# Choosing ScalarE's pair of score tiles from the heads that VectorE's open quad does not need

## The chip, the cores and the metric

The kernel runs on one core of a Trainium2 chip. The metric is device time in microseconds (us) of one execution; the time before is the median of five executions. A profile is one execution recorded by the hardware profiler: it has a time of its own, and a span from its first to its last instruction.

## The reference

Two independent results stand side by side in the output, each 2048 x 640. The first is a spectral filter: a two-dimensional real FFT, a product with complex weights, and the inverse. The second is softmax attention with 32 heads of 20 columns:

```python
X = rfft2(x); y = irfft2(X * (w_r + 1j * w_i))            # output columns 0..639
q, k, v = split(x @ wqkv)                                  # S=2048, D=640, H=32, Dh=20
p = softmax(einsum("bhqd,bhkd->bhqk", q, k) * Dh ** -0.5)
b = einsum("bhqk,bhkd->bhqd", p, v).reshape(B, S, D) @ wo  # output columns 640..1279
```

## The kernel before

**Tiles of the attention.** A unit is one group of four heads (g, 8 of them) and 512 queries (qc, 4 of them): 32 units, worked through in the order of UNITS. Within a unit, one score tile is 128 keys (kt, 16 of them) by 512 queries of one head (j, 0 to 3), one PSUM bank in float32. There are 32 x 16 x 4 = 2048 such tiles. The four tiles of one unit and one kt are called a quad here. A head has 20 columns padded to 32 partitions, so the four heads of a quad lie on four different 32-partition row groups of TensorE, and tiles of different j can be multiplied at the same time (score_mm, L814 to L817).

**Two engines take exponentials.** ScalarE takes tiles in pairs: one ACTIVATE over two neighbouring banks (L1413) makes 128 x 1024 float16 values in a ring of 14 slots. VectorE makes an approximation by integer arithmetic: each tile is clamped from PSUM to int16 (L950, called p1); once the four tiles of its quad are there, two passes over 128 x 2048 (L993, p2, and L992, p3) make two shifted copies, which are read as float16. The values of that quad are scaled once for this (L1000, 128 x 96, called vs). All tiles of a VectorE quad must be from one quad (the assertion at L998).

**PSUM.** Banks 0 and 1, and 2 and 3, are the two sets that ScalarE's pairs alternate between (SETS). Banks 4 to 7 are shared by VectorE's tiles, the accumulator of the value product, and the matmuls of everything else.

**TensorE.** It writes scores (L816: three forms of call: a pair for ScalarE, tiles for VectorE that ride in the same call window as a pair, and tiles for VectorE alone), value products (L1071: four 32-column matmuls side by side are a wave, one wave for each ScalarE quad and three for each VectorE quad), and the background: projections, the filter's stages (L1738, L1821, L1925, L1977) and the output projection (L1217). A value product is only written when all four tiles of a quad are there (pv_waves, L1013).

**The order of the work.** It is decided while the program is built. Class KB walks through a simulated time with a cost for each instruction; at each step every free engine takes what is ready (run, L1574). What comes out are five fixed lists of instructions, one for each engine, with semaphore waits; on the chip each engine works through its list in order. For TensorE the first choice is always ScalarE's next pair (try_act_fill, L864). It takes the pair from pick_set (L793): first the remaining tiles of quads that ScalarE has opened (aq), then new quads. Then, while VectorE has little queued (dve_wants, L925: less than 2.0 us of work, 1.6 us for a second tile, and not all of the shared banks taken), up to two of VectorE's tiles ride along, as far as their heads differ from those of the pair:

```python
            dt = self.pick_dve_tile(set(t[2] for t in tiles), dts)
...
        if self.dq:
            for t in self.dq:
                if t[2] not in bad_j and all(t[2] != d[0][2] for d in dts):
                    return t
            return None
```

Here dq holds the remaining tiles of the quad that VectorE has opened, t[2] is the head, and bad_j are the heads of ScalarE's pair. So a VectorE quad with, say, only heads 0 and 1 left cannot go on beside a pair of heads 0 and 1. Lone VectorE tiles are written by try_dve_fill (L1457) when TensorE has room.

Of the kernel before, what the change touches and what calls it, by code (L numbers as in the profile page):

```python
# [297 lines left out]
class KB:  # L298
# [565 lines left out]
    def try_act_fill(self):  # L864
        if self.ua >= NU:
            return False
        banks = self.SETS[self.grp]
        if any(self.bank_owner[b] is not None for b in banks):
            return False
        if len(self.sets) >= 2:  # L870
            return False
        if self.P.peek("pe", w=[("ps", b) for b in banks]) > self.now:
            return False
        tiles = self.pick_set(len(banks))
        if not tiles:
            return False
        left = sum(4 * len(q) for q in self.qs[self.ua:self.ua + 2]) + len(self.aq)
        if len(tiles) < len(banks) and left > len(tiles) and self.act_started and not self.starved():
            return False
        for t in tiles:  # L880
            self.take_tile(t)
        bl = banks[:len(tiles)]
        rk = set()
        for u, kt, j in tiles:
            rk.update(self.kq_keys(u, kt))
        dts = []
        while len(tiles) + len(dts) < 4 and self.dve_wants(len(dts)):
            db = self.free_bank()
            if db is None:
                break  # L890
            dt = self.pick_dve_tile(set(t[2] for t in tiles), dts)
            if dt is None:
                break
            dts.append((dt, db))
            self.dve_take(dt, db)
        wk = [("ps", b) for b in bl]

        def fn(e):
            inst = None
            for (u, kt, j), b in zip(tiles, bl):  # L900
                inst = self.score_mm(e, u, kt, j, b)
            return inst
        n = len(tiles)
        self.put("pe", fn, 216.0 + 4.0 * (n - 1), r=list(rk), w=wk, name="fillA", mode="S")
        for b in bl:
            self.bank_owner[b] = "act"
        self.sets.append((tiles, bl, self.grp))
        self.grp ^= 1
        self.act_started = True
        self.act_tiles += n  # L910
        for dt, db in dts:
            self.dve_fill(dt, db, 4.0)
        return True
# [1314 lines left out]
```

## Time and profile before

| what | us |
|---|---|
| median of five executions (758.14 to 759.6) | 758.99 |
| the profiled execution, its own time | 756.96 |
| its span | 755.2 |
| busy: PE 722.2, ACT 729.6, DVE 674.3, POOL 132.7 | |
| first exponential of ScalarE starts | 12.52 |
| last exponential of ScalarE ends | 743.5 |

PE is TensorE's matmuls, PEld its weight loads, ACT is ScalarE, DVE VectorE, POOL GpSimd, SP the engine that issues most transfers. Busy time is the union of the recorded instructions of an engine. A recorded instruction can overlap the next one of its engine, so the step from one start to the next, called the pitch below, can be shorter than the recorded duration. Idle time is put down to what ended it. The granted clock of TensorE was 1.00 throughout.

### The profile page before, as it was taken

What the parts mean: (1) busy time and instruction counts of PE and PEld (TensorE: products, weight loads), DVE (VectorE), ACT (ScalarE), POOL (GpSimd) and SP (SyncE); (2) the same over time, 40 slices, a digit from 0 to 9 for tenths busy, and PEclk for the clock granted to TensorE, in tenths of its full rate; (3) what the DMA queues carried; (4) which work ended last, traced back from release to release, by engine and by line L of the source; (5) the groups of instructions that cost most, each with busy time, mean ns of one, the idle gap of its engine ahead of it and who ended that gap; (6) DMA issues with size and microseconds to landing.
All of it is one profiled execution on the core that took longest, in us unless ns stands there. A gap on an engine that the chain in (4) does not pass through costs nothing.

```text
span 755.2 us, 16333 instructions
## 1 busy us (share of the span) xinstructions
PE 722.2 (96%) x6488; PEld 232.0 (31%) x6537; DVE 674.3 (89%) x1259; ACT 729.6 (97%) x797; POOL 132.7 (18%) x141
## 2 busy tenths in 40 slices
PE   8999999999999999999999999999999999999997
PEld 4422332423322222232223333322222233333233
DVE  3698999999899999999988899999898998898995
ACT  5899999999999999999999999999999999999995
POOL 7398740000000100003020021100000000000000
PEclk9999999999999999999999999999999999999999
DMA  9022331102012126013010111130010211111101
GB/s 312 23 69 86 103 97 41 40 7 61 22 37 55 49 74 230 22 47 116 18 49 11 56 51 38 24 110 21 21 46 19 89 36 55 38 52 37 43 20 39
DMA packets 43504, 44.67 MB, mean 59 GB/s; under 512 B 16741, under 2 KB 36583, under 8 KB 43167
## 3 DMA queue, kind: packets, MB, share of 16 engines
q1 hardware_dynamic: 42654, 42.25, 18.6%
q0 software_dynamic: 768, 1.32, 0.7%
q8 instruction: 53, 0.87, 0.5%
q14 instruction: 29, 0.23, 0.1%
HBM read 28.47 MB, written 8.36 MB: 49 GB/s over the span
## 4 chain that ended last, share of the span: by engine, by line
ACT 63%; PE 26%; DVE 9%; issue 1%; DVEq 0%
ACT arena L1413 63%; PE ps L816 9%; PE ps L1071 7%; DVE arena L950 3%; PE ps L1821 2%; PE ps L649 2%; PE ps L1217 2%; PE ps L698 1%; DVE arena L992 1%; PE ps L620 1%; DVE arena L993 1%; DVE arena L1853 1%; DVE arena L1000 1%; PE ps L1977 1%; PE ps L1738 1%
## 5 line engine op out<-in xcount | busy, mean ns | idle before, releaser
L1413 ACT ACTIVATE arena<-ps 128x1024 f16<-128x1024 f32 x784 | 722.4, 1117 | 9.1 <-PE ps L816 7.4
L950 DVE TENSOR_SCALAR arena<-ps 128x512 int16<-128x512 f32 x480 | 320.3, 682 | 32.0 <-PE ps L816 28.4
L816 PE MATMUL ps<-arena 32*128 32x512 bf16 x2048 | 308.7, 384 | 13.8 <-ACT arena L1413 8.9
L1071 PE MATMUL ps<-arena 128*32 128x512 f16 x3008 | 235.5, 385 | 3.0 <-DVE arena L1000 1.0
L816 PEld LDWEIGHTS ps<-arena 32*128 32x128 bf16 x2048 | 76.3, 91 | 291.9 <-ACT arena L1413 268.3
L1123 POOL TENSOR_TENSOR arena<-arena 128x512 bf16<-128x512 f32 x30 | 40.4, 1348 | 512.3 <-DMA arena<-rd 512.3
L992 DVE TENSOR_SCALAR arena<-arena 128x2048 int16<-128x2048 int16 x120 | 89.4, 745 | 3.8 <-PE ps L1071 3.2
L993 DVE TENSOR_SCALAR arena<-arena 128x2048 int16<-128x2048 int16 x120 | 86.4, 720 | 0.6
L1071 PEld LDWEIGHTS ps<-arena 128*32 128x32 bf16 x3008 | 51.0, 94 | 97.3 <-issue 65.4
L649 PE MATMUL ps<-arena 128*128 128x512 bf16 x148 | 44.4, 383 | 2.6 <-issue 2.3
L1821 PE MATMUL ps<-arena 128*128 128x322 bf16 (+1 forms) x198 | 38.2, 304 | 0.7 <-issue 0.2
L1977 PE MATMUL ps<-arena 128*128 128x320 bf16 (+1 forms) x192 | 35.7, 302 | 0.0
L698 PE MATMUL ps<-arena 128*128 128x160 bf16 x320 | 31.5, 234 | 1.2 <-DVE arena L950 0.5
L1000 DVE TENSOR_SCALAR arena<-arena 128x96 bf16<-128x96 bf16 x120 | 31.2, 260 | 0.0
L1853 DVE TENSOR_TENSOR arena<-ps,arena 128x644 bf16<-128x644 f32 (+1 forms) x34 | 27.9, 821 | 3.2 <-PE ps L1821 2.8
L1925 PE MATMUL ps<-arena 128*128 128x512 bf16 (+3 forms) x122 | 29.2, 332 | 1.5 <-issue 1.4
L1217 PE MATMUL ps<-arena 128*128 128x320 bf16 (+1 forms) x152 | 28.8, 302 | 0.6 <-DVE arena L950 0.6
L698 PEld LDWEIGHTS ps<-arena 128*128 128x128 bf16 x320 | 21.3, 98 | 14.5 <-issue 9.8
L1102 DVE COPY arena<-ps 128x512 f32<-128x512 f32 (+1 forms) x33 | 21.9, 667 | 2.4 <-PE ps L1071 2.3
L661 DVE TENSOR_SCALAR arena<-ps 128x512 bf16<-128x512 f32 x34 | 23.2, 682 | 0.6 <-PE ps L649 0.4
L1738 PE MATMUL ps<-arena 128*128 128x512 bf16 x70 | 21.4, 383 | 1.6 <-issue 1.3
L704 DVE CAST arena<-ps 128x320 bf16<-128x320 f32 x32 | 15.5, 487 | 7.2 <-PE ps L698 7.1
(82 smaller groups left out, 366.9 us busy)
## 6 DMA issues: line engine op xcount, KB each, us to landing
arena<-rd SPq DMA_DIRECT2D x120, 64.0 KB
out_dram<-arena SPq DMA_DIRECT2D x32, 160.0 KB
arena<-in_A_x_dram SPq DMA_DIRECT2D x16, 160.0 KB
xs<-arena SPq DMA_DIRECT2D x16, 160.0 KB
arena<-xs SPq DMA_DIRECT2D x4, 640.0 KB
arena<-arena SPq DMA_DIRECT2D x105, 20.0 KB
arena<-ct SPq DMA_DIRECT2D x2, 1024.0 KB
arena<-ct SPq DMA_DIRECT2D x4, 512.0 KB
```

Source lines behind the costliest of these rows:

```text
L649: return lambda e: e.matmul(o, l, r_, start=(cc == 0), stop=(cc == 4))
L698: return lambda e: e.matmul(o, l, r_, start=st, stop=(c == 4), skip_group_check=True)
L816: return e.matmul(self.ps[:, bank, :], self.KT[32 * j:32 * j + 32, g, kt * 128:(kt + 1) * 128], self.QT[32 * j:32 * j + 32, g, qc * 512:(q ...
L950: return e.tensor_scalar(o, in_, 0.0, 31744.0, ALU.max, ALU.min)
L992: self.dve_push([(lambda e, en: e.tensor_scalar(Ii, Ii, SH2, 0.0, ALU.subtract, ALU.max), occ, ik + pk, ik, [], "p3")], lambda: push(self. ...
L993: ops = [(lambda e, en: e.tensor_scalar(Gi, Ii, SH1, 0.0, ALU.subtract, ALU.max), occ, ik, [("G", b)], [], "p2")]
L1071: inst = e.matmul(self.ps[32 * j:32 * j + 32, bank, :], v_, p_, start=s_, stop=False, tile_position=(0, 32 * j), skip_group_check=True)
L1123: self.pool_op(lambda e: e.tensor_tensor(on, of, bc, ALU.mult), 1600.0, r=pk + [("bcu", u, j) for j in range(4)] + [("bc", j) for j in ran ...
L1217: return lambda e: e.matmul(o, ot[0:M, c, qb * 128:(qb + 1) * 128], self.wo[0:M, c, half * 320:(half + 1) * 320], start=(c == 0), stop=(c ...
L1413: self.put("act", lambda e: e.activation(o, in_, AF.Exp, bias=ACT_BIAS, scale=ACT_SCALE), 0.8333 * 512 * n + 60.0, r=[("ps", b) for b in b ...
L1821: return lambda e: e.matmul(o, lhs, r_, start=st, stop=sp)
L1977: return lambda e: e.matmul(o, l, r_, start=(n == 0), stop=(n == 5))
```

## The change

Six lines go into try_act_fill, after a pair has been picked and before it is taken. If VectorE has an open quad and wants a tile, ScalarE's pair is picked again with the heads of VectorE's next two tiles excluded; if that gives no full pair, with the head of the next one excluded. The other pair is used only if, with it, ScalarE has at most two quads open.

```diff
         tiles = self.pick_set(len(banks))
         if not tiles:
             return False
+        if self.dq and self.dve_wants(0):
+            for k in (2, 1):
+                alt = self.pick_set(len(banks), [t[2] for t in self.dq[:k]])
+                if len(alt) == len(banks) and len({t[:2] for t in self.aq + alt}) <= 2:
+                    tiles = alt
+                    break
         left = sum(4 * len(q) for q in self.qs[self.ua:self.ua + 2]) + len(self.aq)
```

The scaled copies of values (L1000) stay on VectorE, as they were. Nothing else is edited; line numbers below L880 grow by six. Because the lists come out of the planner, the order of every engine's list changes from about the first tens of microseconds on.

## The prediction

> **What bounds the kernel now.** I began with the page: busy shares, then the costliest groups.
>
> ```profile
> PE 722.2 (96%) x6488; PEld 232.0 (31%) x6537; DVE 674.3 (89%) x1259; ACT 729.6 (97%) x797; POOL 132.7 (18%) x141
> ...
> L1413 ACT ACTIVATE arena<-ps 128x1024 f16<-128x1024 f32 x784 | 722.4, 1117 | 9.1 <-PE ps L816 7.4
> L950 DVE TENSOR_SCALAR arena<-ps 128x512 int16<-128x512 f32 x480 | 320.3, 682 | 32.0 <-PE ps L816 28.4
> ...
> L992 DVE TENSOR_SCALAR arena<-arena 128x2048 int16<-128x2048 int16 x120 | 89.4, 745 | 3.8 <-PE ps L1071 3.2
> L993 DVE TENSOR_SCALAR arena<-arena 128x2048 int16<-128x2048 int16 x120 | 86.4, 720 | 0.6
> ```
>
> ScalarE's exponentials leave it idle for 9.1 us only. VectorE's clamps (L950) waited 32.0 us, 28.4 of them for TensorE to write a score: that is the wait the change aims at. The means mislead: 784 x 1.117 us is 876, more than the span, so the records overlap. The timeline of ScalarE gives the pitch, and the chain of waits agrees:
>
> ```profile
> 497.57 245.97 ACT L1413 ACTIVATE arena<-ps 128x1024 f16<-128x1024 f32 x268 [0.56 <-PE ps L816]
> ```
>
> ```profile
> 227.97 95.47 ACT arena L1413 x104
> ```
>
> (245.97 - 1.12) / 267 = 0.917 us; 95.47 / 104 = 0.918. So the exponentials need 783 x 0.917 + 1.12 = 719.1 us, and ran from 12.52 to 743.50, 731.0 us: 11.9 us were lost. The span is 12.5 of start, 731.0, and 11.7 of tail.
>
> TensorE and VectorE read in the same way, from the timeline:
>
> ```profile
> 560.24 0.39 PE L816 MATMUL ps<-arena 32*128 32x512 bf16 x2
> 560.55 0.62 PE L1071 MATMUL ps<-arena 128*32 128x512 f16 x8
> 561.10 0.39 PE L816 MATMUL ps<-arena 32*128 32x512 bf16 x2
> 561.42 0.82 PE L1925 MATMUL ps<-arena 128*128 128x512 bf16 x3
> ```
>
> ```profile
> 278.88 0.18 DVE L1000 TENSOR_SCALAR arena<-arena 128x96 bf16<-128x96 bf16 x1
> 279.04 0.69 DVE L950 TENSOR_SCALAR arena<-ps 128x512 int16<-128x512 f32 x1
> 279.65 0.68 DVE L993 TENSOR_SCALAR arena<-arena 128x2048 int16<-128x2048 int16 x1
> 280.25 1.28 DVE L950 TENSOR_SCALAR arena<-ps 128x512 int16<-128x512 f32 x2
> 281.62 0.69 DVE L992 TENSOR_SCALAR arena<-arena 128x2048 int16<-128x2048 int16 x1
> 282.23 0.68 DVE L950 TENSOR_SCALAR arena<-ps 128x512 int16<-128x512 f32 x1
> ```
>
> A pair's two score matmuls and the step to the next kind take 0.31 us; two value waves and a step 0.55; so 0.216 for a slot (score call or wave) and about 0.10 for each change of kind. On VectorE: L950 0.60, L993 0.60, L992 0.61, L1000 0.14: a quad is 4 x 0.60 + 0.60 + 0.61 + 0.14 = 3.75 us.
>
> Last, the windows: start, score phase in three, tail.
>
> ```profile
> core 0: us, PE busy (x) PEld busy (x) DVE busy (x) ACT busy (x) POOL busy (x), PEclk, DMA share, GB/s
> 0.00:12.52 12.52, 9.23 (x68) 4.92 (x69) 5.62 (x11) 4.85 (x7) 11.99 (x16) 1.00 0.85 276
> 12.52:220.00 207.48, 198.89 (x1886) 68.57 (x1906) 181.39 (x317) 202.02 (x219) 72.30 (x77) 1.00 0.22 63
> 220.00:560.00 340.00, 326.18 (x2852) 96.94 (x2874) 314.67 (x582) 336.95 (x367) 37.54 (x41) 1.00 0.20 58
> 560.00:743.50 183.50, 180.11 (x1626) 56.42 (x1628) 168.32 (x335) 183.42 (x201) 10.91 (x8) 1.00 0.13 41
> 743.50:755.20 11.70, 7.75 (x65) 5.11 (x62) 4.35 (x16) 2.39 (x7) 0.00 (x0) 1.00 0.18 61
> ```
>
> VectorE idles 26.1 + 25.3 + 15.2 = 66.6 us of the score phase; ScalarE loses most before 220 us and between 380 and 500. ScalarE bounds, by a small margin over TensorE.
>
> [...]
>
> **The change part by part.** Built but not run, the changed kernel's lists can be counted against the old ones.
>
> *ScalarE.* 776 exponentials in place of 784: minus 8 x 0.917 = 7.3 us if it stays as dense.
>
> *VectorE.* 496 clamps for 480, and 124 for 120 of L992, L993 and L1000: four more quads, 4 x 3.75 = 15.0 us. They must come out of idle time: the full gain needs VectorE's idle to fall from 66.6 to 66.6 - 15.0 - 7.3 = 44.3 us, of which the 28.4 us of waiting for scores could give most. 14 of the 16 extra tiles stand beside ScalarE's 241st to 560th exponential, about 237 to 533 us before; there VectorE had some 22 us idle (25.3 x 296 / 340) and gets 14 / 4 x 3.75 = 13.1 us more, so it comes to about 97% busy. If that cover were missing, all 15.0 us would lie open, which is more than the gain.
>
> *TensorE.* 32 more value matmuls, 8 waves, 8 x 0.216 = 1.7 us; 8 score pairs fewer, minus 1.7; changes of kind 1594 to 1609, 15 x 0.10 = 1.5; keep-warm matmuls 44 to 42, minus 0.4. Summing the list at these prices between ScalarE's fills, from the tenth on: 676.7 us for 774 exponentials (709.8 of ScalarE), after it 677.4 for 766 (702.4): 95.3% becomes 96.4%. The total is covered by ScalarE, the bunching not wholly. Leaving out the start, which is alike, three fills in a row need over 0.3 us more than three exponentials at one place before and at some nine after, by 0.3 to 0.65 us, together about 4. Two banks per set and two sets absorb a part (a fill is due 0.9 us ahead); I take half, 2 us of new ScalarE idle, between 0 and 4.
>
> *Order of heads.* Before, all 784 pairs were heads 0 and 1 or 2 and 3 of one quad, so a quad was done in two exponentials. After, 333 of 776 pairs come from two quads, and a quad's halves span 1 to 4 steps, 2.3 on average; 38 take four. Value products wait for whole quads, so ring slots are held some 1.3 x 0.917 = 1.2 us longer on average. The ring is seven pairs, 6.4 us. The trace shows only 0.3 us in which ScalarE waited for a value product (L1071), so there is room; I take 0.3 us more, between 0 and 2. A VectorE quad is handed over within 4.34 exponentials on average (538 / 124) instead of 4.64, and lone VectorE fills fall from 7 to 2: the mechanism works as said.
>
> *Queues.* SP issues the same transfers and POOL the same work, some at other places. POOL's largest wait (512.3 us, for the broadcast sums) shows that their results have long slack, so I price this at 0, within plus or minus 1. The tail has the same instructions; VectorE's last pass now comes ahead of ScalarE's last exponential, not after it: 0, minus 0.5 to plus 0.5. No wait is added by hand; what queues behind a late value wave is ScalarE's next fill, in TensorE's list.
>
> Sum: 755.2 - 7.3 + 2.0 + 0.3 = 750.2 of span; the profiled execution's time 756.96 - 5.0 = 752.0. The profiled execution was 2.0 below the median, so the median becomes 758.99 - 5.0 = **754.0**.
>
> **The rivals.**
>
> *Full gain.* ScalarE stays as dense: 758.99 - 7.3 = 751.7; if VectorE's better feed also spares some of the 11.9 us lost, 750. For it: in the 20 us windows where VectorE was busy for over 19.2, ScalarE still ran at 19.9 on average. Against it: TensorE is bunched more.
>
> *The gain is paid back, no change.* VectorE at 97% is late with clamps and evictions, value waves wait for it in TensorE's list, fills wait behind them: 7.3 us of new ScalarE idle, 759.0. For it: L1071's weight loads already wait for L950 51 times, 12.5 us. [...]
>
> *Slower: the ring becomes the bound.* If the mixed pairs keep a quad open for four steps and its value wave two or three more, the seven pairs of the ring are full and ScalarE waits. Each of the 38 quads of four steps may cost up to 0.3 us and each of the 116 of three 0.05: 17 us at most. It decides once the added wait exceeds 7.3 us, that is from about 0.2 us for each of the 38; at two thirds of the most, 11 us, 762.7 comes out. Against it: ScalarE's waits for L1071 are 0.3 us now.
>
> That the change does nothing is excluded by the counts.
>
> **How the numbers follow.** A measurement of this kernel can tell 0.2% (1.5 us) from no change. Partial gain (752.5 to 757): 0.48; full gain or better (749.5 to 752.5): 0.23; paid back (757 to 760.5): 0.15; slower (over 760.5): 0.14. The first two are faster by over 0.2%, the third is split: faster 0.73, same 0.12, slower 0.15. The range reaches from 750.3 (full gain with a bit of spared loss) to 760.6, where the slower case starts. The likeliest case alone has 752.5 to 757.
>
> **What would show it.** Right: L1413's pitch still 0.917 in long runs, its idle before 9 to 13 us, the score phase about 726 us long; L950's wait for L816 down from 28.4 to under 20; VectorE at about 690 us busy, 92%. Full gain: idle of L1413 at 9 or below. Paid back: L1413's idle at 14 or more, released by L816, with more waiting of L1071 for VectorE. The ring: L1413 waits for L1071 by several us. Wrong altogether: a longer tail, or a clock below 1.00.

## The result, and the profile after

The changed kernel takes 764.67 us (median of 22 executions, 759.53 to 768.23), against 758.79 for the kernel before (43 executions): the ratio is 1.0066, with a 95% interval of 1.0054 to 1.0079. It is slower. The profiled execution took 765.79 us with a span of 762.3. Lines below the change have moved by six: L1413 is now L1419, L950 is L956, L992 and L993 are L998 and L999, L1071 is L1077.

The page of the changed kernel, busy shares and costliest groups:

```profile
PE 728.3 (96%) x6522; PEld 234.1 (31%) x6567; DVE 686.8 (90%) x1287; ACT 726.2 (95%) x789; POOL 134.0 (18%) x141
...
L1419 ACT ACTIVATE arena<-ps 128x1024 f16<-128x1024 f32 x776 | 719.0, 1086 | 19.5 <-PE ps L816 12.0
L956 DVE TENSOR_SCALAR arena<-ps 128x512 int16<-128x512 f32 x496 | 330.1, 682 | 27.9 <-PE ps L816 23.7
```

There are eight exponentials fewer, as counted, but their idle time before has gone from 9.1 to 19.5 us. VectorE is not full: it is busy for 686.8 of 762.3 us. Who ScalarE waited for, from its list of waits:

```profile
ACT arena L1419 <- PE ps L816: 12.0, 23, 2.3
...
ACT arena L1419 <- PE ps L1077: 4.4, 12, 0.8
```

Columns are us in total, times, and the longest. Before, the waits for value products were these:

```profile
ACT arena L1413 <- PE ps L1071: 0.3, 1, 0.3
```

From the start of the first exponential (13.04 us) to the end of the last (751.03) it is 738.0 us. At the pitch of before 776 exponentials need 775 x 0.917 + 1.12 = 711.8, so 26.2 us are lost there in this profile, where 11.9 were.

One thing is quite new. Here are windows of 4 us around the start of the filter's second stage (L1827), in the changed kernel:

```profile
core 0: us, PE busy (x) PEld busy (x) DVE busy (x) ACT busy (x) POOL busy (x), PEclk, DMA share, GB/s
380.00:384.00 4.00, 3.64 (x38) 1.06 (x36) 3.88 (x8) 3.30 (x5) 3.13 (x5) 1.00 0.32 83
384.00:388.00 4.00, 2.02 (x16) 0.55 (x14) 2.19 (x4) 2.77 (x4) 0.95 (x1) 0.96 0.32 86
388.00:392.00 4.00, 4.00 (x25) 0.97 (x21) 1.90 (x4) 3.01 (x4) 0.00 (x0) 0.50 0.02 4
392.00:396.00 4.00, 4.00 (x32) 0.98 (x29) 2.70 (x5) 2.80 (x3) 0.00 (x0) 0.69 0.01 2
396.00:400.00 4.00, 4.00 (x41) 1.35 (x38) 3.70 (x8) 4.00 (x6) 0.00 (x0) 1.00 0.20 53
400.00:404.00 4.00, 3.53 (x28) 1.08 (x26) 3.97 (x8) 4.00 (x5) 1.27 (x1) 1.00 0.06 19
404.00:408.00 4.00, 3.67 (x20) 0.87 (x18) 3.61 (x7) 2.46 (x3) 0.00 (x0) 0.59 0.08 19
408.00:412.00 4.00, 4.00 (x29) 0.71 (x27) 2.17 (x4) 3.06 (x3) 0.00 (x0) 0.56 0.00 0
```

TensorE was busy for only 2.02 of the 4 us from 384 on, and then its granted clock fell to one half and came back. It fell again at 404, without so empty a window: TensorE was busy for 3.53 of the 4 us from 400 on, but for only 0.73 of the 1.5 from 403.0 to 404.5. The kernel before, in the same place and in its emptiest such window of the score phase:

```profile
384.00:388.00 4.00, 3.15 (x34) 0.91 (x30) 2.34 (x6) 3.20 (x4) 1.11 (x1) 1.00 0.26 66
388.00:392.00 4.00, 3.99 (x36) 1.42 (x34) 3.66 (x8) 4.00 (x5) 0.00 (x0) 1.00 0.01 4
...
152.00:156.00 4.00, 2.99 (x33) 1.06 (x32) 3.78 (x7) 3.47 (x5) 0.35 (x1) 1.00 0.08 19
```

It stumbles there too, but TensorE stays at 3.15 of 4 us, and at 2.99 from 152 on, and keeps its clock in this profile. At half clock the round of fill, value product and fill takes longer than an exponential. TensorE's timeline there, changed kernel:

```profile
390.33 0.61 PE L816 MATMUL ps<-arena 32*128 32x512 bf16 x2
390.87 1.04 PE L1077 MATMUL ps<-arena 128*32 128x512 f16 x8
391.84 0.61 PE L816 MATMUL ps<-arena 32*128 32x512 bf16 x3
392.38 1.05 PE L1077 MATMUL ps<-arena 128*32 128x512 f16 x8
393.36 0.61 PE L816 MATMUL ps<-arena 32*128 32x512 bf16 x3
```

One fill and two waves took 0.86 us at full clock before (560.24 to 561.10); here it is 1.51 us (390.33 to 391.84), against the 0.917 of an exponential. A tile of VectorE that rides along adds nothing to a fill that shows: from the start of a fill to that of the value product it is 0.54 us with two scores (390.33) and with three (391.84), and in the kernel before, at full clock, 0.31 with two (560.24), 0.32 with three (562.18) and 0.32 with four (115.93). From 380 to 416 us ScalarE started 32 exponentials where the kernel before started 39: 7 x 0.917 = 6.4 us in 36. The rest of the new loss in this profile is spread over the score phase.

**Time and clock of every execution.** The mean granted clock is known for each execution, not only the profiled one. In 24 executions of the changed kernel, profiled ones among them, it runs from 0.988 to 1.000, and time follows it closely (correlation 0.94): 759.53 us in the one at 1.000, 768.23 in one at 0.989. A straight line through time and clock, read at 1.00, estimates the cost of the order alone; the rest of the median goes with the clock. The same is done below for each kernel, with an interval from resampling its executions, and once more with the recorded span in place of the time:

| kernel | exponentials | median us | mean clock | line at clock 1.00 (95%) | the same for the span |
|---|---|---|---|---|---|
| before (139 executions) | 784 | 758.9 | 0.9973 | 757.8 (757.5 to 758.0) | 756.0 (755.7 to 756.2) |
| the change (24) | 776 | 764.7 | 0.9935 | 759.8 (759.1 to 760.5) | 756.5 (755.9 to 757.1) |

Medians, mean clocks and lines leave out executions over 1.5% above the fastest of their kernel: four of 20 of the variant one_quad below and one of 13 of nokeep, all at a mean clock of 0.960 to 0.983.

So of the 5.8 us, 2.0 are lost at full clock and 3.8 with the clock (764.7 - 759.8 = 4.9, less 1.1 before). The 3.8 is a remainder of medians: by the slopes of the two lines (0.66 us for 0.001 of clock after, 0.48 before), the mean clocks account for 4.3 - 1.3 = 3.0 of it. A line alone does not say which comes first, the lower clock or the lateness; the runs with fewer and with more keep-warm matmuls below bear on that.

Of the 2.0 at full clock, only 0.5 lies within the recorded span. An execution of the kernel before takes 1.8 us longer than its span (1.76 to 1.94), one of the changed kernel 3.1 on average (2.35 to 3.7), 3.2 by the lines. These 1.4 us lie where the profile has no instruction of the kernel, and what takes them is open.

### The profile page after: what moved, and what is told of

Read it like the earlier page. It is cut to its first block, busy times and chain, and to the rows that moved or that the text cites. A ratio compares the mean times of both kernels' runs of the same rounds, so it can differ in the third digit from the quotient of the medians.

```text
span 762.3 us, 16409 instructions
## 1 busy us (share of the span) xinstructions
PE 728.3 (96%) x6522; PEld 234.1 (31%) x6567; DVE 686.8 (90%) x1287; ACT 726.2 (95%) x789; POOL 134.0 (18%) x141
## 5 line engine op out<-in xcount | busy, mean ns | idle before, releaser
L1419 ACT ACTIVATE arena<-ps 128x1024 f16<-128x1024 f32 x776 | 719.0, 1086 | 19.5 <-PE ps L816 12.0
L956 DVE TENSOR_SCALAR arena<-ps 128x512 int16<-128x512 f32 x496 | 330.1, 682 | 27.9 <-PE ps L816 23.7
L816 PE MATMUL ps<-arena 32*128 32x512 bf16 x2048 | 307.9, 387 | 14.6 <-ACT arena L1419 9.8
L1077 PE MATMUL ps<-arena 128*32 128x512 f16 x3040 | 243.8, 388 | 4.3 <-DVE arena L998 1.8
L816 PEld LDWEIGHTS ps<-arena 32*128 32x128 bf16 x2048 | 75.8, 91 | 285.9 <-ACT arena L1419 247.9
L998 DVE TENSOR_SCALAR arena<-arena 128x2048 int16<-128x2048 int16 x124 | 95.0, 766 | 7.6 <-PE ps L1077 6.5
L999 DVE TENSOR_SCALAR arena<-arena 128x2048 int16<-128x2048 int16 x124 | 89.5, 722 | 0.6
L1077 PEld LDWEIGHTS ps<-arena 128*32 128x32 bf16 x3040 | 52.9, 95 | 106.9 <-issue 74.9
L1827 PE MATMUL ps<-arena 128*128 128x322 bf16 (+1 forms) x198 | 39.6, 315 | 0.1
L1006 DVE TENSOR_SCALAR arena<-arena 128x96 bf16<-128x96 bf16 x124 | 28.2, 228 | 0.0
```

Of the source, the lines that this page charges most:

```text
L816: return e.matmul(self.ps[:, bank, :], self.KT[32 * j:32 * j + 32, g, kt * 128:(kt + 1) * 128], self.QT[32 * j:32 * j + 32, g, qc * 512:(q ...
L956: return e.tensor_scalar(o, in_, 0.0, 31744.0, ALU.max, ALU.min)
L998: self.dve_push([(lambda e, en: e.tensor_scalar(Ii, Ii, SH2, 0.0, ALU.subtract, ALU.max), occ, ik + pk, ik, [], "p3")], lambda: push(self. ...
L999: ops = [(lambda e, en: e.tensor_scalar(Gi, Ii, SH1, 0.0, ALU.subtract, ALU.max), occ, ik, [("G", b)], [], "p2")]
L1077: inst = e.matmul(self.ps[32 * j:32 * j + 32, bank, :], v_, p_, start=s_, stop=False, tile_position=(0, 32 * j), skip_group_check=True)
L1419: self.put("act", lambda e: e.activation(o, in_, AF.Exp, bias=ACT_BIAS, scale=ACT_SCALE), 0.8333 * 512 * n + 60.0, r=[("ps", b) for b in b ...
```

## The experiments

Three theories stood against each other. *Ring*: pairs from two quads keep quads open, value products come later, ring slots are freed later. In the order of the lists, 160 slots are read five or six exponentials after they were written (the ring holds seven pairs), against 38 before. *Clock*: the new order leaves gaps in TensorE's work, and its clock is halved after them. *Chance*: any newly planned order loses against the old one.

**No mixed pairs (one_quad).**

```diff
-                if len(alt) == len(banks) and len({t[:2] for t in self.aq + alt}) <= 2:
+                if len(alt) == len(banks) and len({t[:2] for t in self.aq + alt}) <= 1:
```

> The other pair is used only if ScalarE then has one quad open, so no pair is mixed (784 exponentials, 120 VectorE quads, every quad done in two pairs; 54 ring slots are read five or six exponentials after they were written, against 38 before the change and 160 with it). If mixing two quads is what costs, this is within 0.2% of the time before (757.3 to 760.3), ScalarE waits for value products under 1 us, and the clock stays at 1.00. If any newly planned order loses against the old one, it is slower, 761 to 765.

762.1 us, ratio 1.0042 (1.0022 to 1.0062); mean clock 0.9968; 759.5 at full clock (757.7 to 761.1). It waits for value products for 0.3 us only, as expected, yet it is slower than before, in the range named for chance, and the clock did not stay up. Its windows show the same fall in another place:

```profile
100.00:104.00 4.00, 2.78 (x27) 0.79 (x26) 3.93 (x7) 2.40 (x4) 3.83 (x5) 0.85 0.15 49
104.00:108.00 4.00, 4.00 (x29) 1.66 (x27) 2.40 (x5) 2.93 (x3) 1.68 (x2) 0.50 0.35 100
```

So mixed pairs are needed neither for a loss nor for a fall of the clock. How its 3.2 us divide is less clear: the line puts 1.7 of them at full clock, with a wide interval, and the mean clock of these executions is hardly below that of before.

**Mixed pairs with an age limit (young).** A pair is refused if it would leave the older open quad unfinished a second time.

```diff
-                if len(alt) == len(banks) and len({t[:2] for t in self.aq + alt}) <= 2:
+                if len(alt) == len(banks) and len({t[:2] for t in self.aq + alt}) <= 2 and self.young(alt):
...
+    def young(self, alt):
+        if not self.aq:
+            return True
+        q = self.aq[0][:2]
+        if self.nfa - self.qopen.get(q, self.nfa) < self.AGE:   # fills since q was opened; AGE = 1
+            return True
+        return all(t in alt for t in self.aq if t[:2] == q)
```

> The change with an age limit: a pair that would leave the older open quad unfinished a second time is not taken (788 exponentials, 118 VectorE quads, 176 mixed pairs, quads done in two or three pairs, 44 ring slots read late). If late value products are what costs, ScalarE's waits for them fall back to under 1 us; four exponentials more than before are 3.7 us, so 759 to 763. If mixing itself costs, whatever its length, it is slower than that, 763 to 768.

759.02 us, ratio 1.0007 (0.9991 to 1.0023), mean clock 0.9969, 757.7 at full clock, with four exponentials more than before. It waits 0.2 us for value products. The expectation of the ring theory holds at its lower end: mixing two quads need not cost anything.

**Only the next tile's head (k1).**

```diff
-            for k in (2, 1):
+            for k in (1,):
```

> Only the head of VectorE's next tile is excluded, not those of its next two (774 exponentials, 125 VectorE quads, 220 mixed pairs, 76 ring slots read late). If late value products and the clock are what costs, this keeps most of the ten exponentials saved, 9.2 us, and pays under half of the change's loss: 752 to 758. If every new order loses, 761 to 766, as the change itself.

751.04 us, ratio 0.9899 (0.9871 to 0.9928), lower than expected, in four executions; it was taken up again below. A new order need not lose.

**The kernel before, planned anew (replan).**

```diff
-    DVE_BACK = 2000.0
+    DVE_BACK = 2400.0
```

> The kernel before with another limit of VectorE's queue (2.4 us in place of 2.0), which leaves the counts as they were (784, 120, no mixed pair, 40 slots read late) and changes only the order. If the loss comes from mixed pairs, 757.3 to 760.3. If any new order loses, by chance in its bunching or its clock, 761 to 765.

756.89 us, ratio 0.9980 (0.9968 to 0.9992), 756.4 at full clock. It is slightly faster, not slower, so a new order does not lose by being new. The spread between orders with nearly the same counts is real, though: 756.4 (replan), 757.7 (young), 757.8 (before) and 759.5 us (one_quad) at full clock. That a part of the change's loss, of the size of this spread, is chance of its order is not excluded by any run.

**The ring alone (ring16).** The five lists of the changed kernel were kept instruction for instruction; only the ring is larger. Room for two slots came from letting GpSimd's normed output (On) lie in the buffer it reads, and the flag's scratch in the broadcast's. The core of the edit, with a comment added:

```diff
+    SLOTS = 16
...
-        self.ring = a.bf(a.take(1024 * self.RING), 512 * self.RING).bitcast(F16)
+        self.ring = a.bf(a.take(1024 * self.SLOTS), 512 * self.SLOTS).bitcast(F16)
...
+        vkeys = keys                       # the planner's 14 slots decide, as before
+        slot = self.pr if self.pr + n <= self.SLOTS else 0
+        keys = [("P", i) for i in range(slot, slot + n)]
+        self.pr = slot + n
```

> The changed kernel with its five lists instruction for instruction as they were, and ScalarE's ring kept in 16 slots in place of 14 (the planner still counts 14), so that only ScalarE's waits for value products change. If the ring is what takes the gain away at full clock, ScalarE's waits for L1077's successor fall from 4.4 us to under 1 and the runs at full clock from 759.8 to about 754; the median to 757 to 760. If the ring doesn't matter, 764 to 766 as the change.

760.33 us, ratio 1.0003 (0.9977 to 1.0029). The list of waits of ScalarE (L1431 is the exponential, L819 the scores, L1841 the filter's second stage) no longer names a value product:

```profile
ACT arena L1431 <- PE ps L819: 14.5, 28, 2.3
...
ACT arena L1431 <- PE ps L1841: 1.2, 1, 1.2
```

At full clock it is 756.1 (755.0 to 756.8), 759.77 - 756.14 = 3.6 us less than the change. The clock is about as it was, 0.9943, so this loss is not the clock's. The full-clock figure is 2 us short of the recovery expected (754). Only 2.2 of the 3.6 us lie in the span (756.5 to 754.3 by the lines): the waits for scores have grown from 12.0 to 14.5 us, so a part of the waiting has moved. The other 1.4 lie outside the span: these executions take 1.8 us longer than their spans, like those of before. The waits of ScalarE do not explain this part, and no run shows what does.

**The control for it (ring16b): the same buffers under the lists of before.**

> The kernel before with the same 16 slots under the same lists. It waited only 0.3 us for value products, so every theory expects 758 to 759.5; it shows what the moved buffers alone do.

759.41 us, ratio 1.0006 (0.9990 to 1.0022). The moved buffers gain nothing by themselves.

**Without keep-warm matmuls (nokeep).** These are matmuls that nothing reads; the planner puts one in where it finds TensorE busy for under 55% of its look-back (WARM). The planner still books their time, and their waits stay, but the 42 matmuls are left out of the list.

```diff
-        self.put("pe", lambda e: e.matmul(o, self.ident, i_, start=True, stop=True), 216.0, ... name="keep")
+        self.put("pe", None, 216.0, ... name="keep")
```

> The changed kernel with its lists as they were but the 42 keep-warm matmuls (L1508) left out, their waits kept; they compute nothing that is read. If TensorE's clock is held up by them, the mean clock falls from 0.9935 to 0.985 or less and the time rises to 768 or more. If they only stand in the way of ScalarE's fills, the time falls by up to their 42 x 0.216 = 9 us, to 756 to 763.

764.8 us (761.1 to 768.4), ratio 1.0082 (1.0060 to 1.0104), mean clock 0.9854. Both effects show, so the median stays between the figures of the two theories. The clock fell by 0.008 with nothing changed but these matmuls, so they do hold it up. At full clock the line reads 757.2 (756.3 to 758.6), 2.6 us under the change; this is an extrapolation, since none of its executions was above 0.992. Windows of its profile, at another new place:

```profile
288.00:292.00 4.00, 2.86 (x28) 0.74 (x28) 3.97 (x8) 3.65 (x5) 0.00 (x0) 0.82 1.04 402
292.00:296.00 4.00, 4.00 (x27) 0.76 (x23) 2.94 (x6) 3.81 (x4) 0.07 (x1) 0.50 0.32 89
```

As at the first fall in the change and in one_quad, the fall to one half comes with or after a window in which TensorE was busy for under 3 of 4 us (2.02, 2.78 and here 2.86); at the second fall in the change it did not (3.53).

**More keep-warm matmuls (warm65).**

```diff
-    WARM = 0.55
+    WARM = 0.65
```

> The changed kernel, planned to keep TensorE at least 65% busy in place of 55% (57 keep-warm matmuls in place of 42; 776 exponentials and 124 VectorE quads as in the change). If about 4 us of the change's loss is the clock, the mean clock rises from 0.9935 to 0.997 or more and the median falls to 760 to 762.5. If the clock only follows from lateness elsewhere, 764 to 766 and the clock as it was.

758.62 us, ratio 0.9997 (0.9981 to 1.0014), mean clock 0.9983; better than expected. One constant gives back 6 us of the change: 1.9 at full clock (757.9), through another order, and 4.1 with the clock, of which the slope accounts for 3.2 (0.0048 at 0.66 us per 0.001). As the order is another, this run alone does not show that the added matmuls raised the clock; nokeep shows it for the order of the change. Its waits for value products are still 5.1 us.

**Both cures (combo): the lists of warm65 in 16 slots.**

> Both cures at once: the lists of the kernel planned for 65% busy, and 16 slots of ring under them. If ring and clock are separate losses, the ring's 3.6 us at full clock comes off the 758.6 of the lists alone: 754 to 756.5, clear of the time before; ScalarE's waits for value products, 5.1 us there, vanish. If the two are one loss, 757.5 to 759.

757.09 us, ratio 0.9975 (0.9963 to 0.9987), mean clock 0.9986, 755.8 at full clock. It is clear of the time before, but between the two ranges expected. No wait for a value product is left, yet ScalarE waits longer for scores. First two lines of warm65, then one of combo (whose profile was at a clock of 0.998, the other at 1.000):

```profile
ACT arena L1419 <- PE ps L816: 5.8, 8, 2.3
ACT arena L1419 <- PE ps L1077: 5.1, 15, 0.9
...
ACT arena L1431 <- PE ps L819: 13.0, 25, 2.3
```

The 16 slots gave 2.0 us at full clock here, not 3.6, and most of it lies outside the span: within it the lines read 754.7 and 754.0, with intervals that overlap. So this run does not decide that the losses are two; the gain of ring16 at an unchanged clock does.

**The rest at full clock (ring16_nokeep): the change's lists in 16 slots and without keep-warm matmuls.**

> The changed kernel's lists in 16 slots and without the 42 keep-warm matmuls (nothing that is read is left out). If the rest of the gain at full clock is lost to TensorE being bunched, the line through time and clock meets full clock at 752 to 753.5, which is the full gain; the median is 758 to 764, since the clock falls. If the rest is lost elsewhere, VectorE for one, the line meets full clock at 755.5 or more.

762.79 us, ratio 1.0038 (1.0011 to 1.0065), mean clock 0.9841; the line at full clock reads 754.0 (752.6 to 754.7), between the two expectations, and again as an extrapolation (no execution above 0.992). So 2.1 us (756.1 - 754.0) go with the keep-warm matmuls. The kernel before has 44 of them, and no run leaves those out, so whether the change pays more for its 42 is not shown. 3.5 us above the full gain (757.8 - 7.3 = 750.5) stay unassigned.

**The narrower choice again (k1_again), and in 16 slots (k1_ring16).**

> The variant that excludes only the head of VectorE's next tile, once more and in more executions. If its 751.0 comes from its own order, 750 to 752.5 again, with a mean clock of 0.998 or more. If it was a chance of few executions at a good clock, 753 to 758.

752.63 us, ratio 0.9919 (0.9897 to 0.9941), six executions, clock 0.9977; at full clock 751.8. That is 0.1 us above the range expected: it is the order, and not a good draw of executions. Whether the order owes it to the milder rule, or to chance of the kind that replan shows, is open. The page of its profile:

```profile
L1419 ACT ACTIVATE arena<-ps 128x1024 f16<-128x1024 f32 x774 | 712.7, 1115 | 8.8 <-PE ps L816 5.8
L956 DVE TENSOR_SCALAR arena<-ps 128x512 int16<-128x512 f32 x500 | 331.6, 680 | 21.5 <-PE ps L816 17.8
```

ScalarE's idle is 8.8 us with ten exponentials fewer, and VectorE's wait for scores is down to 17.8: what the prediction described as the full gain.

> The same variant's lists with 16 slots of ring. Its profile showed 1.5 us of waits for value products, two of them, 1.2 us of it in one place, and 76 slots read late. If late value products are what separates the two variants, there is little left to gain: 749.5 to 751. If k1 still loses as much to its ring as the change did, 746.5 to 748.5.

750.78 us, ratio 0.9914 (0.9889 to 0.9940), 750.8 at full clock. Little is left for the ring, about 1 us, within the uncertainty of the two. Either form is the fastest kernel found, about 0.8 to 1% under the kernel before.

## Why the prediction was wrong

The forecast was 754.0 us, range 750.3 to 760.6; 764.67 lies outside it and on the other side of the time before. What failed is the loss side of its sum: against the 7.3 us gained it set 2.3 (2.0 for TensorE's bunching, 0.3 for the order of heads) and nothing for the clock or for time outside the span, where the runs show 13.0.

- *The counts were right, and the price of an exponential nearly so.* There were eight fewer, and the longest run after steps at (148.96 - 1.05) / 160 = 0.924 us (161 exponentials from 577.80 us on), against 0.917. VectorE, at 90%, did not become the bound of the whole, and the tail within the span did not grow. But VectorE's wait for scores only fell to 23.7 us, not under 20. Of the signs named, the idle time of the paid-back case came (19.5 us before L1419, 12.0 of it released by L816), but not its mechanism: value products waited less for VectorE's clamps than before (10.6 us in 45 waits, 12.5 in 51 before). That of the ring came in part (4.4 us). One reading was loose: the two steps of TensorE, 0.31 and 0.55 us, solve to 0.24 for a slot and 0.07 for a change of kind; 0.216 is the planner's own cost. This moves the sum by well under 1 us.
- *The clock: a term that was missing.* The prediction took 1.00 throughout from one profile and named a lower clock only as a sign of being "wrong altogether", with no price and no chance. The kernel before already ran at 0.9973 on average, which its one profiled execution at 1.000 did not show, and the new lists at 0.9935. That is 3.0 to 3.8 of the 10.7 us missed.
- *The order of heads was mis-sized.* The term was 0.3 us, between 0 and 2; ring16 gave back 3.6, 2.2 of it in the span. The average (slots held 1.2 us longer of 6.4) was a poor figure to look at. How many slots are read in the last two steps before they are written again does better: 38, 44 and 54 such reads went with 0.3, 0.2 and 0.3 us of waiting for value products (before, young, one_quad), 76 with 1.5 and 2.2 (k1, twice), 160 with 4.4; but replan's 40 went with 1.5. The rival on the slow side was this very mechanism. Its price of 11 us was too high: the kernel did become slower, but with the ring as one of several causes.
- *The time outside the span was taken as fixed.* The sum carries the 1.8 us between span and time over to the changed kernel. They became 3.2 by the lines. Nokeep and warm65 show the same (3.2 and 3.0 on average), the forms of all three with 16 slots 1.8 to 1.9, and every other kernel here 1.8; the cause is open.
- *TensorE's bunching was mis-sized, as far as can be told.* "I take half, 2 us": what is missing from the full gain at full clock once the ring is cured is 756.1 - 750.5 = 5.6 us. 2.1 of them go with keep-warm matmuls. For the remaining 3.5 the waits name TensorE's scores, but no run isolates what delays them.
- *The sum.* 7.3 gained; 2.2 + 1.4 + 5.6 + 3.8 = 13.0 lost; +5.7 us, measured +5.9 (764.67 - 758.79). It has to close nearly, since 5.6 and 3.8 are remainders.

What stays open besides is why k1, with the same kind of mixed pairs, has so little of these losses, and which feature of an order brings on a fall of the clock at one place and not at another.

## What to carry to other kernels

Where a fixed order leaves two engines over 95% full, count not only the work that it saves but the margin of every buffer: how many reads fall in the last steps before reuse. Take the mean clock of many executions, not of one profile, before calling TensorE's clock a constant; a line through time and clock estimates an order's own cost apart from what goes with the clock. Compare the time of an execution with its recorded span, before and after: what lies outside it shows in no list of waits. When a choice rule helps in principle and the result is worse, try its milder form: here, excluding one head in place of two turned +0.7% into -0.8 to -1%.

## What the runs showed of the hardware

TensorE's clock fell to one half after stretches in which it was less busy, but not idle: 2.02 of 4 us in the change, 2.78 in one_quad, 2.86 in nokeep, and 0.73 of 1.5 us at the second fall in the change. No threshold comes out of such windows: the kernel before kept its clock at 2.99 of 4 us, one_quad at 2.85 (from 392 us on) and nokeep at 2.83 (from 268), and the records hold fewer matmuls than weight loads (6522 and 6567 in the page of the change). The windows right after the first fall read 0.50 in all three kernels (from 388 us on in the change, 104 in one_quad, 292 in nokeep). One and the same list, that of the change, ran at anything from 0.988 to 1.000 in 24 executions; what decides between these is not shown. In the change, 0.001 less of mean clock went with 0.66 us; in the kernel before, with 0.48 us. By estimate, 0.001 of mean clock is about 1.5 us at one half in a span of 760 (0.001 x 760 / 0.5).
